# An attention and MLP kernel: C v for four heads at once, and the order and banks of two output tiles

## The chip, the cores and the metric

The kernel runs on one core of a Trainium2 chip. The time of a run is device time in microseconds (us). Profiles come from one profiled execution; its span runs from the first to the last instruction. Engines: PE is TensorE (matmul; PEld are its weight loads), DVE is VectorE, ACT is ScalarE, POOL is GpSimd and SP is SyncE. L420 means line 420 of the kernel before.

## The reference, cut to what matters

Eight batches of eight heads, 576 tokens, head size 64; landmarks are means of 18 tokens, so 32 per head. Attention is approximated by three softmaxes and an iterated inverse, and a two-layer MLP follows on the 4608 tokens:

```python
A = sm(q, k_lm); Bm = sm(q_lm, k_lm); C = sm(q_lm, k)      # 576x32, 32x32, 32x576 per head
Z = Bm^T / (norm1(Bm) * norminf(Bm) + 1e-6)
for _ in range(6): Z = 2 * Z - Z @ Bm @ Z
x = (A @ Z @ C @ v)                                        # heads side by side: 4608 x 512
h = x @ w_in                                               # 512 -> 2048
out = relu(h)**2 @ w_out                                   # 2048 -> 512
```

## The kernel before

The kernel never forms x. For each batch it forms G, which is Z C v times w_in for each head (8 heads of 32 landmarks: two halves of 128 rows by 2048), and then h^T = G^T A^T, so that the first MLP layer contracts over landmarks.

**Two interleaved streams.** For batch b the outer loop runs `mlp_in(b, f)` for 16 blocks f of 128 hidden units: four matmuls of 288 columns (L572) into an `h` tile, a relu on ScalarE into `r` (L576, three buffers) and its square on VectorE into `gT` (L577). Then `mlp_out` runs the output tiles: each 16 matmuls of 512 columns (L590) against `w_out_bf`, a copy by ScalarE (L595) and a store from ScalarE's queue. Tiles 0 to 3 belong to an even batch, 4 to 8 to the odd one after it. Between these steps, generators advance `attention(b + 1)`, and the tiles of the batch before during `mlp_in`. Output matmuls fill TensorE while attention's short chains wait.

**Order.** Batch 0's attention has nothing to hide behind; PE, DVE and ACT run it in program order (`tc.manual_schedule`). Elsewhere a list scheduler of the compiler orders each engine's queue by program order as priority and by when it believes that operands and buffers are ready; the queue is then fixed, and an engine waits for the instruction at its head. `tc.issue_after(x)` keeps the instructions of a block behind x on x's engine.

**PSUM.** Eight banks: tag `h` has two buffers of two banks, tag `n` three of one bank (all of attention's small products), tag `o` a single bank. Output tiles take turns: tile 0 and tile 4 use an `h` buffer (the name `ops2` in the code; in the profile ops_910 and so on), tiles 2 and 6 an `n` bank, others the single bank. In the last batch tiles 4, 6 and 8 use `h`.

**Attention of one batch.** Heads come in pairs p (rows 0 to 63 and 64 to 127 of a transposed tile; i is the head within its pair). `segment_means` (L236) gives landmark means in a block-diagonal `BD`; `scores` (L359) gives exp of A's and C's scores in `EA` and `EC`, `tails` those of the last 64 tokens; `a_sums` (L384) and `a_rows` (L391) normalize A on VectorE, `a_transposed` (L401, L405) turns it into `AT`. The inverse runs as three joint steps (L308, L311), a last one (L318) and two Newton steps (L328, L331, L338, L341). `c_values` multiplies C by v: per group qd of four heads and token block c, a matmul of 64 columns with the head's 32 weight columns, into the head's own 32 partitions, and one of a single column of ones for the row sums; 80 matmuls a batch. VectorE then divides (L425, L426). Its result and Z give `WT` (L528, L531), and `WT` with `w_in_bf` gives G in four chunks (L546). `side` is a list of steps put between the inverse's steps; each entry runs at one of them.

**Loads.** Batch 0's k and q come from SP's queue. POOL's queue brings, in this order: a first piece of w_in, v of batch 0, the other three pieces of w_in, k and q of batch 1 (`qkt` are the tails, `raw` the rest), four pieces of w_out, v of batch 1; later batches' loads follow, and wait for their buffers there: v of batch b + 2 for C v of batch b. VectorE brings `raw` into token order (`nat`, L181).

Of the kernel before, what the change touches and what calls it, by code (L numbers as in the profile page):

```python
# [34 lines left out]
def kernel(  # L35
# [103 lines left out]
    def load_rest(after):  # L139

        def w_in(j):

            r0, f0 = 256 * (j % 2), 1024 * (j // 2)
            return nc.gpsimd.dma_start(
                w_in_bf[64 * (j % 2):64 * (j % 2) + 64, :, f0:f0 + 1024],
                moe_w_in[r0:r0 + 256, f0:f0 + 1024].rearrange("(j d) f -> d j f", d=D),
            )

        with tc.issue_after(masked.ins):
            one = w_in(0)  # L150
        tc.add_manual_dep(
            one.ins, after.ins.name,
            mybir.DependencyInfo(mybir.DependencyClass.Sync, mybir.DependencyReason.DATA),
            reason="q first")
        with tc.issue_after(one.ins):
            load_v(0, loaded[0])
            for j in range(1, 4):
                w_in(j)
            load_qk(1, loaded[1])
            for j in range(4):  # L160
                nc.gpsimd.dma_start(
                    w_out_bf[:, 4 * j:4 * j + 4, :],
                    moe_w_out[512 * j:512 * j + 512, :].rearrange("(ft fp) c -> fp ft c", fp=P),
                )
            load_v(1, loaded[1])
# [32 lines left out]
    def attention(b: int, R: dict):  # L198
# [155 lines left out]
        def scores(nm, qd):  # L354
            sc = ntile([P, NC4, 2, 2, M])
            for j in range(2):
                p = 2 * qd + j
                for c in range(NC4):
                    nc.tensor.matmul(sc[:, c, j, :, :],  # L359
                                     lhsT=X[nm + "T"][:, c, p, :],  # L360
                                     rhs=BD[:, 1 if nm == "q" else 0, p, 0:64],
                                     start=True, stop=True)
            nc.scalar.activation((EA if nm == "q" else EC)[:, qd, 0:NC4, :],  # L363
                                 sc.rearrange("p c j i m -> p c (j i m)"), AF.Exp, scale=SCALE)

        def tails():
            tl = ntile([P, NPAIR, 2, 2 * M])
            for p in range(NPAIR):
                nc.tensor.matmul(tl[:, p, :, :], lhsT=X["tT"][:, p, :], rhs=BD[:, :, p, 0:64],
                                 start=True, stop=True)  # L370
            nc.scalar.activation(
                EA[0:TAIL, :, NC4, :].rearrange("p q (j x) -> p q j x", j=2),
                tl[0:TAIL, :, 1, :].rearrange("p (q j) x -> p q j x", j=2), AF.Exp, scale=SCALE)
            nc.scalar.activation(
                ect[P - TAIL:P, :, :].rearrange("p q (i x) -> p (q i) x", i=2),
                tl[P - TAIL:P, :, 0, :], AF.Exp, scale=SCALE)
# [30 lines left out]
        cvb = small.tile([P, 2, D], BF16, tag="cvb", name="cvb")  # L407

        def c_values():

            cv = ntile([P, 2, D + 1])
            for qd in range(2):
                for c in range(NC4 + 1):
                    for lo, hi in ((0, D), (D, D + 1)):
                        for a in range(4):
                            h = 4 * qd + a
                            lh = EC[:, qd, c, :] if c < NC4 else ect[:, qd, :]
                            rv = (ones_bf[:] if lo else
                                  X["vm"][:, h, c, :] if c < NC4 else X["vt"][:, h, :])
                            nc.tensor.matmul(  # L420
                                cv[M * a:M * a + M, qd, lo:hi], lhsT=lh[:, M * a:M * a + M], rhs=rv,
                                start=(qd == 0 and c == 0 and lo == 0), stop=(c == NC4),
                                skip_group_check=True)
            rc2 = small.tile([P, 2], F32, tag="rc2", name="rc2")
            nc.vector.reciprocal(rc2[:], cv[:, :, D])  # L425
            nc.vector.tensor_tensor(cvb[:], cv[:, :, 0:D],  # L426
                                    rc2[:, :].unsqueeze(2).to_broadcast([P, 2, D]), ALU.mult)

        act, dve = nc.scalar.copy, nc.vector.tensor_copy
        if first:  # L430
# [22 lines left out]
            side = [[(scores, "q", 1), (a_sums, 0, 0)],  # L453
                    [(tails,), (a_sums, 1, 0)],
                    [(scores, "k", 1), (a_sums, 0, 1)],
                    [(a_sums, 1, 1), (c_values,)],
                    [(a_rows, 0, 0), (a_rows, 0, 1)],
                    [(a_transposed, 0)],
                    [(a_rows, 1, 0), (a_rows, 1, 1)],
                    [(a_transposed, 1)]]  # L460
        else:
# [11 lines left out]
            if b < DMA_T:  # L473
# [10 lines left out]
                    [(a_sums, 1), (a_transposed, 0)], [(c_values,)],  # L484
                    [(a_rows, 1)], [(a_transposed, 1)]]
# [40 lines left out]
        wt = ntile([P, 2, P])  # L526
        for qd in range(2):
            nc.tensor.matmul(wt[:, qd, :], lhsT=cvb.rearrange("p q d -> p (q d)"), rhs=zt[:, qd, :],  # L528
                             start=True, stop=True)
        WT = small.tile([P, 2, P], BF16, tag="WT", name="WT")  # L530
# [6 lines left out]
        for n in range(4):  # L537
            with tc.issue_after(mark[0].ins) if n == 2 and mark else nullcontext():
# [5 lines left out]
                for p in range(NPAIR):  # L544
                    for i in range(2):
                        nc.tensor.matmul(g[i][M * p:M * p + M, :],  # L546
                                         lhsT=WT[64 * i:64 * i + 64, i, M * p:M * p + M],
# [17 lines left out]
    mark = []  # L565

    def mlp_in(b, f, AT, G, gT):
        o = (b % 2) * S
        h = psum.tile([P, 2, 512], F32, tag="h", bufs=2, name="h")
        for qd in range(2):  # L570
            for j in range(2):
                nc.tensor.matmul(h[:, j, 0:HALF], lhsT=G[:, qd, f * P:(f + 1) * P],  # L572
                                 rhs=AT[:, qd, j * HALF:(j + 1) * HALF],
                                 start=(qd == 0), stop=(qd == 1))
# [4 lines left out]
    def mlp_out(b, gT):  # L579

        b0 = b - b % 2
        for t in range(0, NC4) if b % 2 == 0 else range(NC4, 9):
            if t % NC4 == 0 and t < 8 or b == B - 1 and t % 2 == 0:
                ops = psum.tile([P, 2, DM], F32, tag="h", bufs=2, name="ops2")[:, 0, :]
            elif t % NC4 == 2 and b < B - 1:
                ops = ntile([P, DM])[:]
            else:
                ops = psum.tile([P, DM], F32, tag="o", bufs=1, name="ops")[:]
            for f in range(NF):
                mark[:] = [nc.tensor.matmul(ops, lhsT=gT[:, f, t * P:t * P + P], rhs=w_out_bf[:, f, :],  # L590
                                            start=(f == 0), stop=(f == NF - 1))]
                if f < NF - 1:
                    yield
            o_sb = mlp.tile([P, DM], F32, tag="o", bufs=3, name="o_sb")
            nc.scalar.copy(o_sb[:], ops)  # L595
            if t == NC4:
                for i in range(2):
                    r0 = (b0 + i) * S + NC4 * P
                    nc.scalar.dma_start(out[r0:r0 + TAIL, :], o_sb[64 * i:64 * i + TAIL, :])
            else:  # L600
                bb, c = (b0, t) if t < NC4 else (b0 + 1, t - NC4 - 1)
                rows = out[bb * S:bb * S + NC4 * P, :].rearrange("(p c) n -> p c n", c=NC4)
                nc.scalar.dma_start(rows[:, c, :], o_sb[:])
            yield
# [82 lines left out]
```

## Time and profile before

| what | value |
|---|---|
| median of 3 runs (range) | 285.64 us (285.49 to 285.65) |
| the profiled execution | 285.64 us |
| its span | 283.9 us |
| PE busy, matmuls | 264.7 us (93%), 3021 |
| DVE busy | 178.7 us (63%) |
| ACT busy | 168.0 us (59%) |
| POOL busy | 42.8 us (15%) |
| C v matmuls (L420) | 640, from 20.9 to 241.5 us |
| HBM read, written | 36.70 MB, 9.44 MB |

Busy time counts an instruction from its start to its end. Matmuls overlap, so that their durations hold latency, and the distance between starts is their pace. A timeline line gives start, duration, engine, line, operation, output and inputs, shapes, how many were merged, and in brackets how long the engine was idle before it and what released it. A line of the list of waits says who waited for whom, and gives the total in us, the number of times and the longest. A line of the chain of waits gives start, us and what.

### The profile page before, as it was taken

To read this page: it belongs to the slowest core of one execution; us is meant where nothing else is said; L and a number is where in the kernel's file an instruction comes from. 1 tells how busy PE (TensorE), PEld (TensorE's weight loads), DVE (VectorE), ACT (ScalarE), POOL (GpSimd) and SP (SyncE) were. 2 spreads that over 40 slices of the span, in tenths; PEclk is the share of its full clock that TensorE was granted. 3 is DMA by queue.
4 is the path that set the end of the run, shared out by engine and by line. 5 is a ranking of instruction groups with operands and counts; after the bars stand their busy time and mean duration, and the time that the engine had idled before them with its cause. 6 is when DMAs were issued, how large, how long until landed. Compare 5 with 4: busy or idle time off the path is not lost.

```text
span 283.9 us, 7223 instructions
## 1 busy us (share of the span) xinstructions
PE 264.7 (93%) x3021; PEld 157.9 (56%) x3021; DVE 178.7 (63%) x427; ACT 168.0 (59%) x312; POOL 42.8 (15%) x66
## 2 busy tenths in 40 slices
PE   2887699999999999999999999999999999999993
PEld 1754476556754666546654666556655666466441
DVE  3688677857795487647884678457965659345100
ACT  1564579357855677357845677367926666467310
POOL 3844222220212111201220120200000000000000
PEclk9979979999999999999999999999999999999999
DMA  7999999998399969994499939971821011120121
GB/s 200 233 204 196 205 204 187 114 211 147 55 135 161 172 105 162 165 187 58 74 192 188 115 81 151 188 134 39 158 57 48 37 39 38 42 74 37 23 88 74
DMA packets 69632, 35.32 MB, mean 124 GB/s; under 512 B 37344, under 2 KB 63968, under 8 KB 69600
## 3 DMA queue, kind: packets, MB, share of 16 engines
q0 software_dynamic: 37696, 17.17, 50.6%
q1 hardware_dynamic: 26656, 8.26, 18.6%
q10 hardware_dynamic: 5248, 9.44, 9.9%
q8 instruction: 23, 0.38, 0.5%
q14 instruction: 9, 0.07, 0.1%
HBM read 36.70 MB, written 9.44 MB: 162 GB/s over the span
## 4 chain that ended last, share of the span: by engine, by line
PE 73%; DMA 11%; ACT 7%; DVE 5%; issue 2%; POOL 1%; ACTq 0%
PE ops L590 21%; PE h L572 16%; PE n L590 9%; DMA w_out_bf<-in_moe_w_out_dram 6%; PE g L546 3%; DMA vm<-in_v_dram 3%; PE n L236 2%; DMA raw<-in_k_dram 2%; ACT r L576 2%; PE n L420 2%; PE n L401 1%; PE ops_3240 L590 1%; PE ops_4350 L590 1%; PE ops_1517 L590 1%; PE ops_910 L590 1%
## 5 line engine op out<-in xcount | busy, mean ns | idle before, releaser
L576 ACT ACTIVATE r<-h 128x576 bf16<-128x576 f32 x128 | 82.2, 653 | 32.8 <-PE h L572 23.2
L590 PE MATMUL ops<-w_out_bf,gT 128*128 128x512 bf16 x304 | 84.0, 379 | 3.2 <-DMA w_out_bf<-in_moe_w_out_dram 2.4
L572 PE MATMUL h<-AT,G 128*128 128x288 bf16 x512 | 84.8, 288 | 0.3 <-ACT G L552 0.3
L577 DVE TENSOR_TENSOR gT<-r 128x576 bf16<-128x576 bf16 x128 | 57.3, 452 | 39.8 <-ACT r L576 39.2
L590 PEld LDWEIGHTS <-gT 128*128 128x128 bf16 x576 | 53.0, 98 | 45.4 <-issue 9.2
L572 PEld LDWEIGHTS <-G 128*128 128x128 bf16 x512 | 47.1, 99 | 19.4 <-issue 1.6
L590 PE MATMUL n<-w_out_bf,gT 128*128 128x512 bf16 x112 | 29.5, 380 | 0.0
L560 DVE CAST G<-g 128x1024 bf16<-128x1024 f32 x14 | 17.1, 1225 | 13.8 <-PE g L546 13.8
L558 ACT CAST G<-g 128x1024 bf16<-128x1024 f32 x14 | 14.2, 1012 | 9.5 <-PE g L546 9.5
L311 DVE SCALAR_TENSOR_TENSOR EY<-EY,n 128x512 bf16<-128x512 bf16 x24 | 16.4, 683 | 4.2 <-PE n L308 3.4
L331 ACT CAST U<-n 128x256 bf16<-128x256 f32 x16 | 6.0, 373 | 21.0 <-PE n L328 21.0
L359 PEld LDWEIGHTS <-T 128*128 128x128 bf16 x256 | 12.3, 99 | 3.9
L103 POOL DMA_DIRECT2D vm<-in_v_dram x8 | 7.1, 883 | 45.9 <-PE n L420 43.8
L595 ACT COPY o_sb<-ops 128x512 f32<-128x512 f32 x19 | 11.1, 585 | 4.4 <-PE ops L590 4.4
L384 DVE TENSOR_REDUCE ra<-EA 128x20 f32<-128x640 f32 (+2 forms) x18 | 12.9, 732 | 0.4
L391 DVE TENSOR_TENSOR an<-EA,rra 128x640 bf16<-128x640 f32 (+2 forms) x18 | 13.1, 738 | 0.0
L84 POOL DMA_DIRECT2D qkt<-in_k_dram x7 | 4.8, 689 | 49.3 <-PE n L236 31.1
L236 PEld LDWEIGHTS <-nat 128*128 128x128 bf16 x256 | 9.9, 97 | 4.1 <-issue 1.1
L363 ACT ACTIVATE EA<-n 128x512 f32<-128x512 f32 x16 | 9.6, 601 | 3.1 <-PE n L359 3.0
L405 ACT COPY AT<-n 128x576 bf16<-128x576 bf16 x9 | 5.7, 638 | 9.0 <-PE n L401 6.3
L363 ACT ACTIVATE EC<-n 128x512 bf16<-128x512 f32 x16 | 9.7, 606 | 2.4 <-PE n L359 2.4
L341 DVE SCALAR_TENSOR_TENSOR vy<-vy,n 128x256 bf16<-128x256 bf16 x16 | 6.5, 408 | 6.5 <-PE n L338 6.4
(177 smaller groups left out, 354.0 us busy)
## 6 DMA issues: line engine op xcount, KB each, us to landing
out_dram<-o_sb ACTq DMA_DIRECT2D x32, 256.0 KB, 2.5
vm<-in_v_dram POOLq DMA_DIRECT2D x8, 512.0 KB, 9.8
raw<-in_k_dram POOLq DMA_DIRECT2D x7, 512.0 KB, 9.1
raw<-in_q_dram POOLq DMA_DIRECT2D x7, 512.0 KB, 13.3
w_in_bf<-in_moe_w_in_dram POOLq DMA_DIRECT2D x4, 512.0 KB, 10.8
w_out_bf<-in_moe_w_out_dram POOLq DMA_DIRECT2D x4, 512.0 KB, 16.2
raw<-in_k_dram SPq DMA_DIRECT2D x1, 1024.0 KB, 6.5
raw<-in_q_dram SPq DMA_DIRECT2D x1, 1024.0 KB, 8.7
```

Of the source, the lines that this page charges most:

```text
L236: nc.tensor.matmul(means[:, ti, p, :], lhsT=src.rearrange("p h d -> p (h d)"), rhs=seg[:, c + (ti if c == NC4 else 0), :], start=(n == 0 i ...
L311: return nc.vector.scalar_tensor_tensor(out=new[:], in0=old[:], scalar=2.0, in1=nv[:], op0=ALU.mult, op1=ALU.subtract)
L359: nc.tensor.matmul(sc[:, c, j, :, :], lhsT=X[nm + "T"][:, c, p, :], rhs=BD[:, 1 if nm == "q" else 0, p, 0:64], start=True, stop=True)
L363: nc.scalar.activation((EA if nm == "q" else EC)[:, qd, 0:NC4, :], sc.rearrange("p c j i m -> p c (j i m)"), AF.Exp, scale=SCALE)
L384: nc.vector.reduce_sum(ras[i][:, lo:hi, :], EA[:, i, lo:hi, :].rearrange("p c (h m) -> p c h m", m=M), axis=AX.X)
L391: nc.vector.tensor_tensor(an[:, i, lo:hi, :].rearrange("p c (h m) -> p c h m", m=M), EA[:, i, lo:hi, :].rearrange("p c (h m) -> p c h m", ...
L558: nc.scalar.copy(dst, gg[:])
L560: nc.vector.tensor_copy(dst, gg[:])
L572: nc.tensor.matmul(h[:, j, 0:HALF], lhsT=G[:, qd, f * P:(f + 1) * P], rhs=AT[:, qd, j * HALF:(j + 1) * HALF], start=(qd == 0), stop=(qd == 1))
L576: nc.scalar.activation(r.rearrange("p (j t) -> p j t", j=2), h[:, :, 0:HALF], AF.Relu)
L577: nc.vector.tensor_tensor(gT[:, f, o:o + S], r[:], r[:], ALU.mult)
L590: mark[:] = [nc.tensor.matmul(ops, lhsT=gT[:, f, t * P:t * P + P], rhs=w_out_bf[:, f, :], start=(f == 0), stop=(f == NF - 1))]
```

## The change

1. C v: `c_values(qd)` multiplies all four heads' v with four heads' weights at once: one matmul of 256 columns and one of a single column of ones per token block, 20 a batch. Of the 256 columns each head's partitions use 64. The division is ScalarE's copy with a scale per partition, one for each qd. The two qd are separate steps in `side`.
2. With it the order of heads within the 128 rows changes from four consecutive heads to i and then pairs: `EA`, the tails, `WT` and the loads of w_in follow (pieces of 512 hidden units for all 128 partitions, not of 1024 for 64), and the lists `side` are written anew.
3. Batch 0's tile 0 takes the single bank, and its first matmul stays behind the matmuls of `mlp_in(0, 9)` on TensorE; tile 1 takes an `h` buffer.
4. The last tile is computed in two halves of 256 columns in the two `h` buffers; the first half is copied by VectorE and stored from SP's queue, the second by ScalarE and stored from its own.

```diff
         def w_in(j):
-            r0, f0 = 256 * (j % 2), 1024 * (j // 2)
             return nc.gpsimd.dma_start(
-                w_in_bf[64 * (j % 2):64 * (j % 2) + 64, :, f0:f0 + 1024],
-                moe_w_in[r0:r0 + 256, f0:f0 + 1024].rearrange("(j d) f -> d j f", d=D),
+                w_in_bf[:, :, j * 512:(j + 1) * 512],
+                moe_w_in[:, j * 512:(j + 1) * 512].rearrange("(kt cp) f -> cp kt f", cp=P),
...
+            if nm == "q":
+                nc.scalar.activation(EA[:, :, 0:NC4, 64 * qd:64 * qd + 64],
+                                     sc.rearrange("p i c j m -> p i c (j m)"), AF.Exp, scale=SCALE)
...
-        def c_values():
-            cv = ntile([P, 2, D + 1])
-            for qd in range(2):
-                for c in range(NC4 + 1):
-                    for lo, hi in ((0, D), (D, D + 1)):
-                        for a in range(4):
...
-                            nc.tensor.matmul(
-                                cv[M * a:M * a + M, qd, lo:hi], lhsT=lh[:, M * a:M * a + M], rhs=rv,
-                                start=(qd == 0 and c == 0 and lo == 0), stop=(c == NC4),
-                                skip_group_check=True)
-            rc2 = small.tile([P, 2], F32, tag="rc2", name="rc2")
-            nc.vector.reciprocal(rc2[:], cv[:, :, D])
-            nc.vector.tensor_tensor(cvb[:], cv[:, :, 0:D],
-                                    rc2[:, :].unsqueeze(2).to_broadcast([P, 2, D]), ALU.mult)
+        def c_values(qd):
+            cv = ntile([P, 4 * D + 1])
+            for c in range(NC4 + 1):
+                if c < NC4:
+                    lh, rv = EC[:, qd, c, :], X["vm"][:, 4 * qd:4 * qd + 4, c, :]
+                else:
+                    lh, rv = ect[:, qd, :], X["vt"][:, 4 * qd:4 * qd + 4, :]
+                nc.tensor.matmul(cv[:, 0:4 * D], lhsT=lh, rhs=rv, start=(c == 0),
+                                 stop=(c == NC4), skip_group_check=True)
+                nc.tensor.matmul(cv[:, 4 * D:4 * D + 1], lhsT=lh, rhs=ones_bf[:], start=False,
+                                 stop=(c == NC4), skip_group_check=True)
+            rc2 = small.tile([P, 1], F32, tag="rc2", name="rc2")
+            nc.vector.reciprocal(rc2[:], cv[:, 4 * D:4 * D + 1])
+            cvb = small.tile([P, 4 * D], BF16, tag="cvb", name="cvb")
+            nc.scalar.activation(cvb[:], cv[:, 0:4 * D], AF.Copy, scale=rc2[:])
+            cvbs[qd] = cvb
...
-            side = [[(scores, "q", 1), (a_sums, 0, 0)],
-                    [(tails,), (a_sums, 1, 0)],
-                    [(scores, "k", 1), (a_sums, 0, 1)],
-                    [(a_sums, 1, 1), (c_values,)],
-                    [(a_rows, 0, 0), (a_rows, 0, 1)],
+            side = [[(scores, "q", 1)],
+                    [(tails,), (a_sums, 0, 0)],
+                    [(a_sums, 0, 1), (scores, "k", 1)],
+                    [(a_rows, 0, 0), (c_values, 0)],
+                    [(a_rows, 0, 1), (a_sums, 1, 0), (c_values, 1)],
                     [(a_transposed, 0)],
-                    [(a_rows, 1, 0), (a_rows, 1, 1)],
+                    [(a_sums, 1, 1), (a_rows, 1, 0), (a_rows, 1, 1)],
                     [(a_transposed, 1)]]
...
             side = [[(scores, "q", 0)], [(scores, "q", 1)], [(tails,)],
                     [(a_sums, 0), (scores, "k", 0)], [(scores, "k", 1), (a_rows, 0)],
-                    [(a_sums, 1), (a_transposed, 0)], [(c_values,)],
-                    [(a_rows, 1)], [(a_transposed, 1)]]
+                    [(c_values, 0)], [(a_sums, 1), (a_transposed, 0)],
+                    [(a_rows, 1), (c_values, 1)], [(a_transposed, 1)]]
...
-        wt = ntile([P, 2, P])
-        for qd in range(2):
-            nc.tensor.matmul(wt[:, qd, :], lhsT=cvb.rearrange("p q d -> p (q d)"), rhs=zt[:, qd, :],
+        wt = ntile([P, NPAIR, 2 * M])
+        for p in range(NPAIR):
+            o = P * (p % 2)
+            nc.tensor.matmul(wt[:, p, :], lhsT=cvbs[p // 2][:, o:o + P],
+                             rhs=zt[:, p // 2, 64 * (p % 2):64 * (p % 2) + 64],
...
+        if (b, f) == (0, 9):
+            begin.append(last)
...
-            if t % NC4 == 0 and t < 8 or b == B - 1 and t % 2 == 0:
-                ops = psum.tile([P, 2, DM], F32, tag="h", bufs=2, name="ops2")[:, 0, :]
+            first, final = (b, t) == (0, 0), (b, t) == (B - 1, 8)
+            if final:
+                halves = [psum.tile([P, 2, DM], F32, tag="h", bufs=2, name="ops2")[:, 0, 0:DM // 2]
+                          for i in range(2)]
+            elif (t % NC4 == 0 and not first and t < 8 or (b, t) == (0, 1)
+                  or b == B - 1 and t % 2 == 0):
+                halves = [psum.tile([P, 2, DM], F32, tag="h", bufs=2, name="ops2")[:, 0, :]]
...
+            n = DM // len(halves)
+            for i, ops in enumerate(halves):
+                for f in range(NF):
+                    with tc.issue_after(begin[0].ins) if first and f == 0 else nullcontext():
+                        mark[:] = [nc.tensor.matmul(ops, lhsT=gT[:, f, t * P:t * P + P],
+                                                    rhs=w_out_bf[:, f, i * n:i * n + n],
+                                                    start=(f == 0), stop=(f == NF - 1))]
...
+                o_h = o_sb[:, i * n:i * n + n]
+                if final and i == 0:
+                    nc.vector.tensor_copy(o_h, ops)
+                else:
+                    nc.scalar.copy(o_h, ops)
+                queue = nc.sync if final and i == 0 else nc.scalar
```

## The prediction

> **What bounds the kernel now.** I read the page's shares and slices, then the waits of TensorE, then the chain of waits, then timelines of the places that the change touches.
>
> ```profile
> PE 264.7 (93%) x3021; PEld 157.9 (56%) x3021; DVE 178.7 (63%) x427; ACT 168.0 (59%) x312; POOL 42.8 (15%) x66
> PE   2887699999999999999999999999999999999993
> PE ops L590 <- DMA w_out_bf<-in_moe_w_out_dram: 2.4, 1, 2.4
> PE n L338 <- ACT U L331: 0.7, 2, 0.5
> ```
>
> TensorE is full from slice 5 on; after its first 10 us its only long wait is one of 2.4 us for the output weights. So from about 48.8 us to the end every TensorE nanosecond added or removed moves the end; before that other things count. The stages by windows (columns: PE, PEld, DVE, ACT, POOL busy; clock, DMA share, GB/s) say the same:
>
> ```profile
> 34.20:48.80 14.60, 13.89 (x152) 10.42 (x152) 10.68 (x30) 11.38 (x23) 4.69 (x6) 0.88 1.47 196
> 48.80:60.80 12.00, 12.00 (x180) 5.65 (x180) 10.29 (x21) 5.93 (x10) 3.55 (x4) 1.00 1.17 152
> 175.80:237.70 61.90, 61.55 (x721) 36.31 (x721) 41.28 (x99) 39.39 (x76) 1.56 (x2) 1.00 0.47 88
> ```
>
> A matmul's own duration contains its latency, so the pace must come from starts. The chain gives it in three lines:
>
> ```profile
> 61.86 0.49 PE n L236 x20
> 259.67 0.98 PE h L572 x8
> 272.76 3.45 PE ops L590 x16
> ```
>
> That is 25 ns for a 32-column matmul, 122 for 288 columns, 216 for 512, hence (122 + 216 points on one line) 109 for 256 columns. The present C v, second batch, by the timeline (its lines between left out):
>
> ```profile
> 52.84 0.38 PE L590 MATMUL ops_910<-w_out_bf,gT 128*128 128x512 bf16 x1
> 53.15 0.21 PE L420 MATMUL n<-vm,EC 128*32 128x64 bf16 x4
> ...
> 53.75 0.20 PE L420 MATMUL n<-ones_bf,ect_91 128*32 128x1 bf16 x4
> 53.88 0.39 PE L590 MATMUL ops_910<-w_out_bf,gT 128*128 128x512 bf16 x1
> ```
>
> 80 small matmuls in four column strips: 53.88 - 52.84 - 0.216 = 0.82 us of TensorE time, some 0.19 of it gaps at both ends. And the first output matmul, which stands early in TensorE's queue:
>
> ```profile
> 31.68 0.69 DVE L181 COPY nat<-raw 128x2048 bf16<-128x2048 bf16 x1 [1.36 <-DMA raw<-in_q_dram]
> 33.43 0.65 ACT L576 ACTIVATE r<-h 128x576 bf16<-128x576 f32 x1 [1.33 <-DVE gT L577]
> 34.30 0.38 PE L590 MATMUL ops<-w_out_bf,gT 128*128 128x512 bf16 x1 [2.40 <-DMA w_out_bf<-in_moe_w_out_dram]
> 35.21 0.65 ACT L576 ACTIVATE r<-h 128x576 bf16<-128x576 f32 x1 [0.97 <-PE h L572]
> ```
>
> The name "ops" is the single bank: it is tile 1, issued ahead of tile 0 (ops_910, from 48.77), because tile 0 has to wait for an h buffer. It blocks the queue until 34.30; four more matmuls of it lie between relu tiles (39.42 to 45.16).
>
> **What the Trainium skill says.** "TensorE: Matmul & The Clock Gate", section "Back-to-back issue gap": 256 columns take 262 cycles, 1 to 64 about 60; that is 109 and 25 ns at 2.4 GHz, which the three lines agree with. "TensorEngine Tiling (Array Packing)", section "Key Properties": changing the tiling mode drains the engine; the 0.19 us of gaps fit. "DMA: Bandwidth & Descriptors", section "Issuing engines are not separate DMA queues": two queues share the same DMA engines; no view of before shows output stores on two queues.
>
> **The change, part by part.**
>
> *C v, batches 1 to 7.* Per batch 10 matmuls of 256 columns and 10 of one column, all at full array width. The one-column matmul is not in the trace; its nearest row is the 32-column one, 25 ns. 10 x (109 + 25) = 1.34 us against 0.82: +0.52 us, seven times = **+3.6 us**, in stretches where TensorE is full. Bounds: one-column matmuls hidden wholly, 7 x (1.09 - 0.82) = +1.9; every one at 62 ns, which the same section gives as the slower issue floor, 7 x 0.89 = +6.2. I take 3.6, since 25 ns was measured with a weight load for each matmul, as here.
>
> *Normalizing C v.* Vector loses its product (0.29 us) and gains one reciprocal of 0.13. Scalar gains two scaled copies of 256 columns a batch. The nearest row is the scaled copy L302, 0.364 for 128 columns; L331 takes 0.372 for 256 without a pointer scale. "ScalarE: Activation LUTs", section "What ACT_TABLE_LOAD costs", prices 0.833 ns an element and 93 ns for such an operand: 0.364 + 0.107 = 0.47, an estimate. That is 0.94 us a batch on an engine busy 59%; in the windows above it has 6 of 12 us free. Cost nothing, covered by output matmuls; but the second copy ends closer to the product that needs it (L528). If TensorE waits there, up to 0.5 us a batch: 0 to +3.
>
> *L528.* Four matmuls of 64 columns for two of 128: nothing. *Scores, tails:* the same elements in another order, nothing; bound +-0.1. *POOL:* v of the batch after next waits for C v, which now ends a step or two later; the raw loads behind it have a batch of slack (some 30 us). Nothing.
>
> *Input weights.* Four loads of 1 KB pieces in place of 2 KB pieces. Two answers on DMA, 18 to 22 us (the old pieces) and 34 to 38 us (output weights, which have the new ones' size):
>
> ```profile
> DMA packets 438, 0.85 MB, mean 212 GB/s; under 512 B 31, under 2 KB 31, under 8 KB 437
> DMA packets 836, 0.84 MB, mean 210 GB/s; under 512 B 29, under 2 KB 835, under 8 KB 835
> ```
>
> Twice the packets, the same bytes per second: 2.1 MB cost 9.9 or 10.0 us, so +0.1 for all behind them.
>
> *Batch 0's attention.* Here the order is written by hand. Vector gets two row sums and both row products (0.38 + 0.28 + 0.53 + 0.42 = 1.6 us) ahead of the last Newton step, where 0.85 stood; Scalar gets C v's copy ahead of U. Laid out with the trace's durations the last step starts at 26.3 instead of 25.38: 0.9 us later to the first G. Cover: Vector stands still for raw q until 31.68, and the first squares lie behind that copy. I take 0; if the cover is gone, +0.9.
>
> *First tile.* Tile 0 gets the single bank and may not start before relu tile 9's matmuls; the wait of 2.4 us goes. What could run in it: the q means (ready at 32.4) and relu tile 4, about 1.0 us of TensorE work; more is not ready, since Scalar waits at 33.43 for Vector's square (three r buffers). Then Scalar's relu at 35.21 can start at 34.08, the next (36.58) at 34.75, and the second batch's landmark chain moves by some 1.5 us. From about 40 us Scalar is nearly full, so that shift lasts: it has 14.60 - 11.38 = 3.2 us idle here, all that can be won. What is late next is the square behind raw q. The displaced output matmuls (5 x 0.216) run later, in time that has to be filled anyway. I take **-1.7 us**; bounds 0 (attention's 0.9 comes back and Vector paces all) and -3.2.
>
> *Last tile.* The last lines of the timeline:
>
> ```profile
> 279.70 0.58 ACT L595 COPY o_sb<-ops_4806 128x512 f32<-128x512 f32 x1 [2.87 <-PE ops_4806 L590]
> 280.32 0.34 ACTq L603 DMA_DIRECT2D out_dram<-o_sb  x1
> ```
>
> 32 matmuls of 109 ns for 16 of 216: +0.04. The final copy takes 0.37 (L331) instead of 0.58: -0.21. The final store is half as large; from issue to the end of the span are 3.6 us, mostly fixed; 128 KB less at the kernel's 200 GB/s or more are at most 0.6 us, I take 0.25. Sum **-0.4**, bounds 0 and -0.8.
>
> **Sum.** +3.6 + 0.1 - 1.7 - 0.4 = +1.6. The profiled execution took 285.64 us (span 283.9 and 1.7 around it), which is also the median of the three runs: 287.2.
>
> **Rivals.** *The early stage wins more than C v loses (faster).* One mechanism: without the block Scalar runs through from 33.4 to 48.8 us and all 3.2 us come forward. With -0.4 at the end it decides against 3.6 when C v costs less than 0.45 a batch: one-column matmuls at 18 ns or less. With 10 x (109 + 10) = 1.19, +0.37 x 7 = +2.6, the time is 285.64 + 2.6 + 0.1 - 3.2 - 0.5 = 284.6. For it: Scalar's idle time. Against it: Vector, not TensorE, releases the relu at 33.43.
>
> *No early gain (slower still).* Attention 0 ends 0.9 later, the schedule hands the freed time to nothing: 285.64 + 3.7 - 0.4 = 288.9. For it: Vector's 10.68 us in that stage and raw q's landing, which don't move.
>
> *C v's copies on Scalar hold L528.* Six full batches by 0.5 on top: 290.2. For it: Scalar runs in program order, relus of 0.65 stand between. Against: no wait at L528 in TensorE's list now.
>
> *The change doesn't do what it says:* tile 0 might still be issued early. The held instruction is the first of its chain, so the rest cannot pass it; if it did start early, the present stall would stay, which is the second rival's time.
>
> **How the numbers follow.** A measurement here tells about 0.2% (0.57 us) from no change. Forecast 0.58, near 287.2, of which 0.05 falls within 286.2; no early gain 0.14 and held L528 0.10, both slower; early stage wins 0.18, of which 0.10 is faster and 0.08 within. So faster 0.10, same 0.13, slower 0.77. The range 285.4 to 290.0 leaves out the best part of the first rival and the worst of the third.
>
> **What would show it.** C v: start to next foreign start near 1.34 us a batch in two pieces; one-column matmuls 25 ns apart. No wait for the output weights in TensorE's list; the relu of 35.21 at about 34.1; the first tile whole before 52 us. Last copy 0.37. The forecast is wrong if C v is not about 0.5 us dearer, if the batch period (61.9 us for two, 175.80 to 237.70) doesn't grow by about 1.0, or if the stage before 48.8 us doesn't shrink.

## The result, and the profile after

| | before | after |
|---|---|---|
| median of runs on one chip (range) | 285.56 us (284.87 to 285.65, 4 runs) | 286.71 us (286.55 to 287.37, 4 runs) |
| ratio, 95% interval | | 1.0050 [1.0028, 1.0072] |
| profiled execution, span | 285.64, 283.9 us | 286.55, 284.8 us |

The change makes the kernel slower by some 1.15 us; 287.2 with a range of 285.4 to 290.0 had been forecast. In the kernel after, lines have moved: the first MLP layer's matmuls are L576, the relu L582, the output matmuls L605, the output copy L614, C v L421 (256 columns) and L423 (one column), G L550.

First the page of after: its shares, and the slices of TensorE and of its granted clock.

```profile
PE 267.1 (94%) x2573; PEld 163.2 (57%) x2573; DVE 179.4 (63%) x428; ACT 174.8 (61%) x328; POOL 43.5 (15%) x66
PE   2967799999999999999999999999999999999995
PEclk9999999999999999999999999999999999999999
```

The number of matmuls falls by 448 (C v -480, the last tile +16, L531 +16) and TensorE is busy 2.4 us *longer*: fewer instructions are not less work. The clock row is worth a look: in after it is 9 throughout. In the page of before it was

```profile
PEclk9979979999999999999999999999999999999999
```

with a 7 in slice 5 counted from 0 (35.5 to 42.6 us; the windows below place it). The other 7, in slice 2, belongs to the start and is also found in profiles without the wait (e10_tile1n). The forecast had not used this row, and it carries much of what follows. One profile shows one execution, and the clock is not the same in all of them; a part below counts them. The list of TensorE's waits no longer has the output weights; of the waits after the start, this is the longest now:

```profile
PE h L576 <- ACT r L582: 1.8, 3, 1.3
```

The timeline of after, in the early stage (Vector's copy of raw q, and the relus of tiles 3 and 4):

```profile
31.23 0.69 DVE L179 COPY nat<-raw 128x2048 bf16<-128x2048 bf16 x1 [1.36 <-DMA raw<-in_q_dram]
32.98 0.65 ACT L582 ACTIVATE r<-h 128x576 bf16<-128x576 f32 x1 [1.26 <-DVE gT L583]
33.80 0.65 ACT L582 ACTIVATE r<-h 128x576 bf16<-128x576 f32 x1
```

The relu of tile 4, which stood at 35.21, 3.53 us behind the copy of raw q, stands at 33.80, 2.57 behind it, and no longer waits for TensorE. The second batch's C v, its first piece:

```profile
51.66 0.27 PE L421 MATMUL n<-vm,EC 128*128 128x256 bf16 x1
51.77 0.17 PE L423 MATMUL n<-ones_bf,EC 128*128 128x1 bf16 x1
51.80 0.27 PE L421 MATMUL n<-vm,EC 128*128 128x256 bf16 x1
...
52.31 0.16 PE L423 MATMUL n<-ones_bf,ect_91 128*128 128x1 bf16 x1
52.34 0.38 PE L605 MATMUL ops_928<-w_out_bf,gT 128*128 128x512 bf16 x1
```

Starts are 110 and 25 to 30 ns apart, five pairs in 52.34 - 51.66 = 0.68 us, so 1.36 us a batch where 0.82 stood. The windows give the price over two whole batches that begin and end at the same places of the program as the window shown of before:

```profile
175.88:238.81 62.93, 62.58 (x604) 37.64 (x604) 41.37 (x99) 41.08 (x80) 1.56 (x2) 1.00 0.52 95
```

62.93 us against 61.90. And the end of the timeline:

```profile
279.70 0.42 DVE L612 COPY o_sb<-ops_4382 128x256 f32<-128x256 f32 x1 [13.54 <-PE ops_4382 L605]
281.39 0.37 ACT L614 COPY o_sb<-ops_4383 128x256 f32<-128x256 f32 x1 [2.91 <-PE ops_4383 L605]
281.79 0.34 ACTq L623 DMA_DIRECT2D out_dram<-o_sb  x1
```

The last copy takes 0.37 us, and from the last store's issue to the end of the span (284.83) it is 3.04 us instead of 3.60.

With four anchors of the timelines the difference of the two profiled executions adds up: Vector's copy of raw q 31.68 and 31.23 us (-0.45); from there to the first h matmul of batch 1 29.09 and 28.37 (-0.72); from there to the last matmul 218.51 and 221.48 (+2.97); from the last matmul to the end 4.64 and 3.75 (-0.89). The sum is +0.91, and the spans are 283.92 and 284.83. The first of these is the landing of a load; over the profiled executions of this study it lay anywhere from 30.86 to 32.08 us with no order by kernel, so I put nothing down to the change there, and measure the early stage from that copy on.

### The profile page after: what moved, and what is told of

It is laid out like the page before. It is cut to its first block, busy times and chain, and to the rows that moved or that the text cites. A ratio compares the mean times of both kernels' runs of the same rounds, so it can differ in the third digit from the quotient of the medians.

```text
span 284.8 us, 6339 instructions
## 1 busy us (share of the span) xinstructions
PE 267.1 (94%) x2573; PEld 163.2 (57%) x2573; DVE 179.4 (63%) x428; ACT 174.8 (61%) x328; POOL 43.5 (15%) x66
## 3 DMA queue, kind: packets, MB, share of 16 engines
q1 hardware_dynamic: 26800, 8.39, 20.2%
## 4 chain that ended last, share of the span: by engine, by line
PE 70%; DMA 14%; DVE 8%; ACT 5%; issue 2%; POOL 0%; ACTq 0%
PE ops L605 20%; PE h L576 16%; DMA raw<-in_q_dram 9%; PE n L605 9%; PE g L550 3%; DMA vm<-in_v_dram 3%; PE n L421 2%; PE n L234 2%; DMA raw<-in_k_dram 2%; ACT r L582 2%; DVE ra L389 2%; DVE gT L583 2%; DVE EY L309 1%; PE ops_3978 L605 1%; PE ops_1950 L605 1%
## 5 line engine op out<-in xcount | busy, mean ns | idle before, releaser
L582 ACT ACTIVATE r<-h 128x576 bf16<-128x576 f32 x128 | 82.1, 653 | 31.0 <-PE h L576 23.4
L576 PE MATMUL h<-AT,G 128*128 128x288 bf16 x512 | 83.8, 286 | 2.1 <-ACT r L582 1.8
L605 PE MATMUL ops<-w_out_bf,gT 128*128 128x512 bf16 x304 | 83.7, 379 | 0.5 <-ACT o_sb L614 0.5
L605 PEld LDWEIGHTS <-gT 128*128 128x128 bf16 x592 | 54.0, 98 | 40.5 <-issue 8.0
L576 PEld LDWEIGHTS <-G 128*128 128x128 bf16 x512 | 46.6, 98 | 20.1 <-issue 2.8
L605 PE MATMUL n<-w_out_bf,gT 128*128 128x512 bf16 x112 | 29.8, 380 | 0.0
L614 ACT COPY o_sb<-ops 128x512 f32<-128x512 f32 x19 | 11.1, 585 | 4.4 <-PE ops L605 4.4
L421 PE MATMUL n<-vm,EC 128*128 128x256 bf16 x64 | 10.8, 270 | 0.0
L306 PE MATMUL n<-EY 128*128 128x256 bf16 x48 | 9.5, 273 | 1.3 <-ACT EY L300 0.5
```

What stands on the lines that cost most here:

```text
L421: nc.tensor.matmul(cv[:, 0:4 * D], lhsT=lh, rhs=rv, start=(c == 0), stop=(c == NC4), skip_group_check=True)
L576: last = nc.tensor.matmul(h[:, j, 0:HALF], lhsT=G[:, qd, f * P:(f + 1) * P], rhs=AT[:, qd, j * HALF:(j + 1) * HALF], start=(qd == 0), stop ...
L582: nc.scalar.activation(r.rearrange("p (j t) -> p j t", j=2), h[:, :, 0:HALF], AF.Relu)
```

## Experiments

Each edit is to the kernel before unless it names another kernel. The ratio is to the kernel before on the same chip (284.69 us for the first four, 284.62 for the second four, 284.19 for the last two); it comes with its interval from all runs, and is not exactly the quotient of the medians.

**The parts alone.** Four kernels: the first tile's change only; the last tile's only; C v's only (with the layout and the lists `side`, but the old tiles); both tiles' without C v's.

```diff
# e1_first: the last tile stays whole
+            first, final = (b, t) == (0, 0), False
# e2_last: the first tile stays as it was
+            first, final = False, (b, t) == (B - 1, 8)
# e3_cv: c_values(qd), order of heads, side of after; mlp_in and mlp_out of before
# e4_tiles: c_values and side of before; mlp_in and mlp_out of after
```

> The kernel before with the first tile's change alone (tile 0 in the single bank behind relu tile 9's matmuls, tile 1 in an h buffer); C v and the last tile as before. Theory A, from the changed kernel's trace (its joint step that stood at 45.07 us starts at 42.58, but the first h tile of the second batch moves only from 60.77 to 59.6): the wait for the output weights goes, the stage gains some 2.5 us by 47 us, and about 1 us of that is given back before 60 us for a reason that has nothing to do with C v. Then this kernel is 1.0 to 1.7 us faster than before. Rival B: what is given back is C v's own new steps; then the gain lasts and it is 2.0 to 2.7 us faster. Rival C: the early stage gains nothing by itself: within 0.4 us.

> The kernel before with the last tile's two halves alone. Traces: from the first matmul of the last tile to the end of the span the changed kernel takes 7.1 us, the kernel before 7.9. Theory: 0.75 us faster, of which 0.2 is the shorter copy and 0.55 the smaller last store. The prediction's own term says 0.4. Rival: the store from SP's queue delays the other by sharing the DMA engines; then 0 to 0.2 us faster.

> The changed kernel with the output tiles of before: C v for four heads at once with all that follows it (order of heads, loads of w_in, ScalarE's division, step lists), but first and last tile as before. Theory A: C v costs 0.52 us of TensorE time a batch and TensorE is full from the second batch on, so 2.6 to 3.7 us slower than before, with 0.53 us more per batch between the fourth tiles of later batches. Rival: some of it is hidden by waits that were there already, 1.5 to 2.5 us. Rival: the division on ScalarE makes the product with Z wait, 4 us or more.

> The kernel before with both output tiles' changes and its own C v: the version that should beat both. Theory A: the sum of the two parts alone, 1.8 to 2.4 us faster than before (283.2 to 283.8). Rival B (early gain lasts without the new C v): 2.8 to 3.5 us faster. Rival: the parts do not add, 1.2 us or less.

| kernel | median us | ratio, 95% interval | span us |
|---|---|---|---|
| e1_first | 284.05 | 0.9985 [0.9969, 1.0001] | 282.8 |
| e2_last | 283.97 | 0.9971 [0.9952, 0.9989] | 282.3 |
| e3_cv | 289.44 | 1.0164 [1.0131, 1.0196] | 287.9 |
| e4_tiles | 283.26 | 0.9951 [0.9930, 0.9971] | 281.4 |

C v's part costs and the last tile's gains; the first tile's gain alone is at the edge of what the runs can tell. Only e2_last came in at its forecast (0.72 us gained). The first tile's change alone gains 0.6 us, and both tiles' 1.4, less than the 1.0 to 1.7 and 1.8 to 2.4 forecast. C v's kernel loses 4.7 us, more than the 2.6 to 3.7 forecast. In size that agrees with the rival that ScalarE's division makes the product with Z wait, but its TensorE list has no wait at that product (L531). Its profile has the wait for the output weights, as before has it. From the copy of raw q to the first h matmul of batch 1 it takes 30.14 us against 29.09, of which one C v explains 0.5; why the rest is lost stays open. From that matmul to the last one, where the start of the kernel plays no part, it takes 221.32 us, and before, e1_first, e2_last and e4_tiles take 218.35 to 218.51: +2.8 to 3.0 us for six batches, 0.47 to 0.49 each; after takes 221.48.

**Without the hold.** The tiles' changes, but tile 0's first matmul is not kept behind relu tile 9.

```diff
-                    with tc.issue_after(begin[0].ins) if first and f == 0 else nullcontext():
+                    with nullcontext():
```

> Both output tiles' changes on the C v of before, but tile 0's first matmul free (no hold behind relu tile 9): banks as in the change, the early matmul back in the queue. Theory A: the hold does the work, the bank only makes room; the wait of 2.3 to 2.5 us for the output weights is back, relu tile 4 starts 3.5 us after the copy of batch 1's q instead of 2.6, and what is left is the last tile's gain less what tile 1 in an h buffer costs: 0.2 us slower to 0.7 us faster than before. Rival B: the single bank for tile 0 brings the gain; then 1.2 us or more faster, as with the hold.

284.47 us, 1.0003 [0.9978, 1.0027], span 284.1. The wait is back in TensorE's list (2.4 us, once), and the gain of the first tile is gone, as theory A had it. So the hold earns it, not the bank.

**Where half of the early gain goes.** Measured from the copy of raw q, the landmark copies of batch 1 (L302; L300 in after) come at +10.42 us in before and +8.39 in after: 2.0 us won. At the first h matmul of batch 1 only 1.0 is left in e4_tiles (+28.12 against +29.09). Two suspects showed in the timelines: tile 1 now sits in an `h` buffer while G is made in the other one, and batch 2's raw q, wanted earlier, has not landed. One experiment leaves out the load of batch 1's v, which stands ahead of that raw q (so its output is another), and one moves tile 1 out of the `h` buffer.

```diff
# e9_tiles_v1: e4_tiles, and in load_v
+        if b == 1:
+            X["vm"] = loaded[0]["vm"]
# e10_tile1n: e4_tiles, and in mlp_out
-            elif (t % NC4 == 0 and not first and t < 8 or (b, t) == (0, 1)
-                  or b == B - 1 and t % 2 == 0):
+            elif t % NC4 == 0 and not first and t < 8 or b == B - 1 and t % 2 == 0:
...
-            elif t % NC4 == 2 and b < B - 1:
+            elif (t in (1, 3) if b == 0 else t % NC4 == 2 and b < B - 1):
```

> Both output tiles' changes on the C v of before; the main part of batch 1's v is not loaded and batch 0's v is used in its place (1 MB less to read, so that batch 1's C v is another product), which takes some 2.6 us out of the queue of loads ahead of batch 2's k and q. Theory D (the late load of batch 2's q gives the gain back: its copy waits 0.3 to 0.5 us on VectorE ahead of W's copy): that wait goes, W's copy comes 0.3 to 0.5 us earlier and the second batch's first h tile 0.4 to 1.0 us earlier than with the tiles' changes alone. Theory H (G's four chunks pass through one h buffer because tile 1 holds the other): the first h tile moves by less than 0.3 us, and the times are within 0.3 us of the version that loads it.

> Both output tiles' changes on the C v of before, with tile 1 of batch 0 in an n bank, tile 2 in the single bank and tile 3 in an n bank, so that no output tile of batch 0 holds an h buffer while G is made. Theory H: G's matmuls stand in two groups of 16 instead of four of 8, two gaps of 0.29 us and a wait for ScalarE's copy go, and the second batch's first h tile comes 0.5 to 1.0 us earlier; 1.9 to 2.4 us faster than before. Theory D: nothing moves, 1.2 to 1.6 us faster as with the tiles' changes alone. Rival: attention lacks n banks; slower than the tiles' changes alone.

e9_tiles_v1: 282.77 us, 0.9941 [0.9923, 0.9958]. e10_tile1n: 282.56 us, 0.9930 [0.9909, 0.9952]. The intervals overlap with that of e4_tiles, so the times don't rank these three, and I go by the traces. G's matmuls in the timeline of after:

```profile
55.30 0.41 PE L550 MATMUL g<-w_in_bf,WT 64*32 64x512 bf16 x8
56.84 0.41 PE L550 MATMUL g<-w_in_bf,WT 64*32 64x512 bf16 x8
57.50 0.41 PE L550 MATMUL g<-w_in_bf,WT 64*32 64x512 bf16 x8
58.60 0.41 PE L550 MATMUL g<-w_in_bf,WT 64*32 64x512 bf16 x8
```

and in that of e10_tile1n:

```profile
54.58 0.62 PE L546 MATMUL g<-w_in_bf,WT 64*32 64x512 bf16 x16
56.54 0.62 PE L546 MATMUL g<-w_in_bf,WT 64*32 64x512 bf16 x16
```

With one `h` buffer G comes in four groups, the last 3.3 us behind the first; with two it comes in two groups, 1.96 apart, as in before (56.95 and 58.91). Groups cost TensorE time: from the start of a group of eight to the next output matmul it is 0.34 us (58.60 to 58.94 in after), of a group of 16 it is 0.56 (54.58 to 55.14 in e10_tile1n), and a gap of about 0.1 us stands ahead of each group. So four groups instead of two cost some 0.4 us. (The gaps of 0.29 us in the expectation are too long: the eight matmuls of a group run side by side, 0.41 us for all of them in the lines above.) The second suspect shows on Vector in e4_tiles, in the copies of batch 2's raw k and q and of W:

```profile
52.74 0.69 DVE L181 COPY nat<-raw 128x2048 bf16<-128x2048 bf16 x1
53.90 0.69 DVE L181 COPY nat<-raw 128x2048 bf16<-128x2048 bf16 x1 [0.47 <-DMA raw<-in_q_dram]
54.51 0.42 DVE L531 CAST WT<-n 128x256 bf16<-128x256 f32 x1
```

The copy of W divides the two. From it to the first h matmul of batch 1, where G is made, it is 4.77 us in e4_tiles and 4.78 in after, 4.35 in e10_tile1n and 4.29 in before: the bank costs 0.4 to 0.5. Ahead of it, Vector waits for raw q 0.47 us in e4_tiles, 0.33 in after and 0.26 in e1_first, and not in before or in e9_tiles_v1, where W's copy comes 0.57 us earlier than in e4_tiles (22.78 us behind the copy of batch 1's raw q, against 23.35). Bank and late load together are nearly all of the 1.0 given back. The first h matmul comes at +27.54 us in e10_tile1n, +27.76 in e9_tiles_v1 and +28.12 in e4_tiles. By itself this anchor tells less: e1_first, which differs from e4_tiles only in the last tile, has +27.91. Theory D had forecast 0.4 to 1.0 us for e9_tiles_v1 and theory H less than 0.3; it is 0.36, between the two: W's copy comes 0.57 us earlier, as D has it, and 0.21 of that is lost again while G is made.

The same banks on the kernel after:

```diff
# e12_after_tile1n: against after
-            elif (t % NC4 == 0 and not first and t < 8 or (b, t) == (0, 1)
-                  or b == B - 1 and t % 2 == 0):
+            elif t % NC4 == 0 and not first and t < 8 or b == B - 1 and t % 2 == 0:
...
-            elif t % NC4 == 2 and b < B - 1:
+            elif (t in (1, 3) if b == 0 else t % NC4 == 2 and b < B - 1):
```

> The changed kernel with the same other banks for batch 0's tiles 1 to 3 (n, single, n). Theory H: 0.5 to 1.0 us faster than the changed kernel, so 0.4 to 0.9 us slower than before. Theory D: as the changed kernel, 1.2 to 1.4 slower than before.

286.54 us, 1.0073 [1.0050, 1.0096]: no gain over after that the runs can tell, and slower than either theory had it. Its G comes in two groups, and from W's copy to the first h matmul it takes 4.28 us, 0.50 less than in after, so the bank is worth here what it is worth with the old C v. But W's copy comes 0.25 us later behind the anchor (23.84 against 23.59), so that only 0.25 is left at the h matmul (+28.12 against +28.37). Its second piece of C v is late there (its reciprocal at +21.83 us, against +21.31); why, stays open.

**The wait or the clock behind it.** In every profile that has the wait for the output weights (before and three of the kernels above), the granted clock is halved for 3.4 us around the end of the wait; in the six others it is not. The windows of before:

```profile
36.00:38.00 2.00, 2.00 (x17) 1.47 (x16) 1.10 (x3) 1.23 (x3) 0.68 (x1) 0.50 1.27 214
```

The column after the five engines is the clock: 0.50. So the 2.0 us may be the wait, or the slow stretch, as I call the 3.4 us at half clock. Two kernels tell these apart. Both are e4_tiles with one extra matmul on the output weights at the old place in TensorE's queue, with q's means and all that follows kept behind it; the second fills the wait with ten matmuls whose operands are long there.

```diff
+        if (b, f) == (0, 4):
+            fill = psum.tile([P, DM], F32, tag="o", bufs=1, name="fill")
+            for i in range(n + 1):    # e13_wait: n = 0, e14_waitfill: n = 10
+                with tc.issue_after(block[-1].ins):
+                    w = w_out_bf if i == n else w_in_bf
+                    block.append(nc.tensor.matmul(fill[:], lhsT=w_in_bf[:, 0, 0:P], rhs=w[:, 0, 0:DM],
+                                                  start=True, stop=True))
...
+            if b > 0 or f == 0 or f > 4:
+                attend((f + 1) * half // NF)
+            elif f == 4:
+                with tc.issue_after(block[-1].ins):
+                    attend(5)
```

> Both tiles' changes with the old C v, plus one extra matmul of 512 columns that uses the first piece of the output weights; it stands in TensorE's queue at the place of the first output matmul of before (three matmuls of h(0,4) ahead of it), and q's means and what follows them stay behind it. So the wait for the output weights is back, and the first tile still stays behind relu tile 9. Times from the start of Vector's copy of raw q. Theory (half the early gain is the wait, half the halved clock after it): relu tile 4 at +3.5, the landmark copies at about +10.4, granted clock halved for about 3.4 us behind the wait, time about 284.5. Rival (the clock costs nothing, the wait alone is the 2.0 us): the same figures for this kernel.

> The kernel with the wait, and ten more matmuls of 512 columns on the input weights directly ahead of the waiting one: 10 x 0.216 = 2.2 us of TensorE work in the time of the wait, so that TensorE is not idle there; all that stands behind it is as late as before. Theory: no halved clock; relu tile 4 still at about +3.5 from Vector's copy of raw q, but the landmark copies at about +9.4, and the time about 0.6 to 1.0 us below the kernel with the wait. Rival: relu tile 4 at +3.5 and the landmark copies at +10.4 as with the wait, and the same time within 0.3 us; the clock dip is then harmless, since Scalar and Vector set the pace there.

The timeline of e13_wait (the extra matmul, the next six of h, relu tile 4, the landmark copies), and then a window in and behind the end of the wait:

```profile
33.54 0.58 PE L575 MATMUL fill<-w_out_bf,w_in_bf 128*128 128x512 bf16 x1 [2.20 <-DMA w_out_bf<-in_moe_w_out_dram]
33.92 1.64 PE L580 MATMUL h<-AT,G 128*128 128x288 bf16 x6
35.12 0.65 ACT L588 ACTIVATE r<-h 128x576 bf16<-128x576 f32 x1 [1.62 <-PE h L580]
41.22 0.63 ACT L302 ACTIVATE EY<-n,rc 128x128 bf16<-128x128 f32 x2
```

```profile
33.60:36.60 3.00, 3.00 (x30) 1.90 (x30) 1.30 (x4) 0.91 (x2) 0.94 (x2) 0.50 1.24 207
```

The same two views of e14_waitfill:

```profile
31.82 2.32 PE L575 MATMUL fill<-w_in_bf 128*128 128x512 bf16 x10
34.40 0.38 PE L575 MATMUL fill<-w_out_bf,w_in_bf 128*128 128x512 bf16 x1 [0.25 <-DMA w_out_bf<-in_moe_w_out_dram]
35.30 0.65 ACT L588 ACTIVATE r<-h 128x576 bf16<-128x576 f32 x1 [0.96 <-PE h L580]
40.50 0.62 ACT L302 ACTIVATE EY<-n,rc 128x128 bf16<-128x128 f32 x2
```

```profile
33.60:36.60 3.00, 2.70 (x40) 1.75 (x39) 2.06 (x6) 1.84 (x5) 0.88 (x1) 1.00 1.24 207
```

With TensorE kept busy, but for 0.25 us, the clock stays at 1.00. The output weights release both kernels 2.6 us behind the copy of raw q (30.94 and 31.77 us). In the filled kernel relu tile 4 is then still at +3.53, as late as in before; yet the landmark copies come at +8.73, against +10.28 with the bare wait and +8.38 in e4_tiles, which has neither. **Of the 1.9 us between e4_tiles and the bare wait, 1.55 are the halved clock and 0.35 the wait** (one profile of each kernel). The theory had said half and half (+9.4 for the filled one); it was right in kind and had the clock's share too small, and the rival, that the clock is harmless, is out. From the copy of raw q to the last matmul it is 248.30 us with the bare wait, 246.75 filled, 246.48 in e4_tiles: the 1.55 lasts to the end. The times, 284.73 us (1.0009 [0.9990, 1.0029]) and 283.80 us (0.9995 [0.9969, 1.0020]), lie in that order, but their intervals overlap; this verdict rests on the traces. All twelve:

| kernel (all from the copy of raw q, us) | wait, halved clock | relu tile 4 | landmark copies | first h of batch 1 |
|---|---|---|---|---|
| before | yes, yes | 3.53 | 10.42 | 29.09 |
| e2_last | yes, yes | 3.68 | 10.39 | 29.07 |
| e3_cv | yes, yes | 4.41 | 10.78 | 30.14 |
| e5_nohold | yes, yes | 3.83 | 10.40 | 29.52 |
| e13_wait | yes, yes | 4.18 | 10.28 | 29.67 |
| e14_waitfill | filled, no | 3.53 | 8.73 | 28.41 |
| e1_first | no, no | 2.57 | 8.39 | 27.91 |
| e4_tiles | no, no | 2.56 | 8.38 | 28.12 |
| e9_tiles_v1 | no, no | 2.56 | 8.38 | 27.76 |
| e10_tile1n | no, no | 2.56 | 8.38 | 27.54 |
| after | no, no | 2.57 | 8.39 | 28.37 |
| e12_after_tile1n | no, no | 2.57 | 8.38 | 28.12 |

**How often the clock falls.** For the experiments the mean clock of every execution is known, not only of the profiled ones. A stretch of 3.4 us at half clock takes 0.006 off a mean over 284 us; the profile of before has two, one at the start, and 0.988. Of the 130 executions of before that were timed beside the experiments, 35 have 0.999 or 1.000, so no such stretch, and a median of 283.75 us; 24 have 0.988 or less, and 285.45; the others lie between. So before does not pay for the slow stretch each time. Eleven executions of e1_first at 0.999 or 1.000 have a median of 283.93 us, the ten of before on the same chip 283.78: there the first tile's change gains nothing, which fits 0.35 won from the wait and 0.4 to 0.5 lost to the bank. Of these executions only the profiled ones were traced, so it isn't shown whether the wait was in those without a slow stretch. One reason is possible if it was: within each profile the clock changes whole multiples of 3.41 us apart (in before at 18.14, 21.56, 35.21 and 38.62 us), wherever the wait ends, from 0.9 us ahead of the slow stretch (before) to 0.4 behind its start (e13_wait). In the 3.41 us ahead of it TensorE was busy for 1.57 us or less in the five profiles that have it, and in the seven others for 2.08 us or more in each such period between 27 and 37 us. Before's:

```profile
31.80:35.21 3.41, 1.01 (x11) 0.75 (x11) 3.03 (x7) 1.12 (x4) 1.12 (x2) 1.00 1.24 205
```

A wait that two such periods share might leave each of them busy enough. No run tests this.

## Why the prediction was right, step by step

*C v, +3.6: held.* It measured 1.36 us a batch where 1.34 was worked out, and the one-column matmul took the 25 to 30 ns that the 32-column row had given. Over whole batches it is 0.47 (six batches) to 0.52 (the two-batch window) each, so 3.3 to 3.6 for seven.

*C v's copies on Scalar, nothing: held.* The copy of 256 columns takes 0.47 us, as estimated, and after's list of TensorE's waits has none at L531 (L528 before), so the rival of a held L528 is refuted.

*Input weights, +0.1: not to be told from nothing.* From Vector's first copy of k to that of batch 1's raw q it is 24.3 us in before and 24.5 to 24.6 in the three kernels with the new pieces, which is the size forecast; but the kernels with the old pieces range from 24.1 to 24.9.

*Batch 0's attention, +0.9 under a cover: held, with 0.6.* At first sight the delay is not there, since the first h tile of batch 0 stands at 27.77 us in after and at 27.76 in before. But in after the first copy of k was 0.6 us earlier (6.72 us against 7.34). The two Newton steps of Vector between which the added work stands show the delay, in before and in after:

```profile
23.63 0.41 DVE L341 SCALAR_TENSOR_TENSOR vy<-vy,n 128x256 bf16<-128x256 bf16 x1
25.38 0.42 DVE L341 SCALAR_TENSOR_TENSOR vy<-vy,n 128x256 bf16<-128x256 bf16 x1
```

```profile
23.01 0.42 DVE L339 SCALAR_TENSOR_TENSOR vy<-vy,n 128x256 bf16<-128x256 bf16 x1 [0.27 <-PE n L336]
25.37 0.41 DVE L339 SCALAR_TENSOR_TENSOR vy<-vy,n 128x256 bf16<-128x256 bf16 x1
```

They are 2.36 us apart instead of 1.75, and so in all three kernels with the new lists. The cover held: behind the copy of raw q, relu tile 4 comes at +2.57 in after as in e1_first, which has the old attention.

*The first tile, -1.7: the size was off and its reason mostly wrong.* The relu moved by 0.96 (3.53 to 2.57) where 1.13 was worked out, and no wait is left; this part was well read. But the prediction said that this shift lasts because Scalar is nearly full from 40 us. e14_waitfill has the relu as late as before and loses only 0.35 us of the early gain. What the change removes, in the profiled execution, is a pause with 3.4 us of half clock at its end; this term, 1.55 us, was not in the sum, although the clock of 0.88 in the first of the windows shown, and the 7 of slice 5 in the clock row, were there to be read. What the prediction missed on the other side is the price of tile 1 in an `h` buffer while G is made, and of raw q of batch 2 landing too late: together 0.9 to 1.0 in e4_tiles. At batch 1's first h matmul, against before, e1_first has -1.18 and e4_tiles -0.97; after has -0.72 with some 0.5 of C v in it, so -1.2. Two missed terms of opposite sign left a forecast of -1.7 only half a microsecond off. That is luck, and there is a second piece of it: the profile of before, from which the forecast was made, is an execution with the slow stretch, and the four it was compared with (284.87 to 285.65 us) are slower than the median of before on any other chip, so that by their times they had it too (their clocks are not known). Against executions without the stretch the change costs more than forecast: eight of e12_after_tile1n, the change with other banks, at 0.999 or 1.000 have a median of 286.52 us, and ten of before on the same chip 283.68, so +2.8.

*The last tile, -0.4: right in kind, too small.* From the last tile's first matmul to the end it is 7.14 us instead of 7.88, -0.74; e2_last by itself has -0.72 in its time. The mis-sized term is the store: -0.56 where 0.25 was taken, close to the bound of 0.6 that had been given (128 KB at 200 GB/s are rather 0.66 us). The copy gave its -0.21.

*The sum.* 3.3 to 3.6, + 0.1, - 1.2, - 0.74 gives +1.5 to +1.8, beside +1.15 by the medians, [0.8, 2.1] by the interval, and +0.9 in the two profiled executions, of which -0.45 is raw q's landing. The "early stage wins more" rival was short of both its conditions: C v was no cheaper than 0.47 a batch, and the early stage gave back half of what it won.

**A better version.** e10_tile1n leaves C v as it was and gives tiles 1 and 3 of batch 0 an `n` bank: 0.9930 [0.9909, 0.9952] of before. Its median is the lowest of the kernels here, though its interval overlaps that of e4_tiles, which was timed on another chip.

## What to carry to other kernels

Price matmuls by their starts in a trace, not by their count: 80 narrow ones cost 0.82 us and 20 wide ones 1.36. Both sets stream about 2600 columns, but the narrow ones ran side by side in four strips: four of them take 0.21 us together in the line at 53.15 of before. When a stall of TensorE goes, look at the clock row behind it, for the slow stretch may have cost more than the stall; if the stall must stay, independent matmuls in it can pay even though their results are thrown away (1.55 us here, by one pair of profiles). And when a tile moves to another bank, ask what else wanted that bank in the time it is held.

## What the runs showed of the hardware

An idle time of 2.2 to 2.5 us, in a TensorE that was nearly full before and after it, went with half the clock for 3.4 us in all five profiles that had it, and none of the seven others had a halved clock there. In e13_wait the slow stretch began when the pause had lasted 1.8 us. The Trainium skill, "TensorE: Matmul & The Clock Gate", section "Part 1: The HAM clock gate", says that the array falls to half its clock after an idle window of about 3.4 us, and that windows run free of the kernel's start. The length of the slow stretch, 3.4 us, agrees, and so do changes of the clock that lie whole multiples of it apart in each profile; that a shorter pause suffices is this case's finding. Whether it does so each time is open: 35 of 130 executions of before had no slow stretch by their mean clock, and whether they had the pause was not traced. With 0.25 us of idle time left (e14_waitfill) the clock stayed full.

Halving the last store from 256 to 128 KB took 0.56 us off the time from its issue to the end (3.60 to 3.04). At the kernel's average of 162 GB/s those bytes would be 0.81 us.
